# Keeping a bounded activation in PSUM, its high part on ACT, and an order planned with the port that DVE and GpSimd share

## Chip, cores and metric

The kernel runs on one core of a Trainium2 chip. The metric is the device time of one execution in microseconds, median of several runs; less is better.

## What is computed

Attention under a block-causal mask, and behind it two feed-forward layers on its output: the first with a quadratic bounded activation, the second with a leaky ReLU.

```python
# q, k, v: (4, 8, 576, 64); w_in: (512, 2048), w_out: (2048, 512) in each layer
scores = np.matmul(q, k.transpose(0, 1, 3, 2)) / np.sqrt(64)
mask = (pos[:, None] // 64) >= (pos[None, :] // 64)
scores = np.where(mask, scores, -1e9)
attn = softmax(scores) @ v
x = attn.transpose(0, 2, 1, 3).reshape(2304, 512)

h = x @ moe_w_in                      # layer 0
g = np.where(h >= 1, h, np.where(h <= -1, 0.0, (h + 1) ** 2 / 4))
x = g @ moe_w_out

h = x @ moe2_w_in                     # layer 1
g = np.maximum(0.01 * h, h)
out = g @ moe2_w_out                  # (2304, 512)
```

The weights are read as 64-bit words that the kernel itself converts to 32-bit floats.

## The kernel before

**Split operands.** In the two layers every operand stands as a high part (rounded to the fp32r type) and a low part (what the rounding left), and a product is three matmuls: high by high, low by high, high by low. A step therefore needs of each activation g the tiles gh and gl, and of each weight its two parts in the tile w.

**Tiles and stages.** Tokens are worked in blocks: layer 0 has seven of 256 and one of 512 tokens, layer 1 four of 512 and one of 256. The hidden dimension of 2048 is cut into 16 chunks of 128. A step of `moe_block` takes one chunk for 512 tokens or two for 256, so that its h is always one PSUM bank of 128x512. A block of 256 tokens has 8 steps, one of 512 has 16. In each step PE computes h (L579: 24 matmuls of 256 columns or 12 of 512) and, behind it, the step before's part of the output y (L618 in layer 0, L625 in layer 1). Between the two the activation is made: in layer 0 by ACT (L589 Relu of half of h and a half, L591 its square) and DVE (L592, the smaller of that and of max(h, 1), into g), in layer 1 by ACT (L596, 0.01 h) and DVE (L598, the maximum, into g). Then POOL copies g rounded into gh (L600) and DVE subtracts gl = g - gh (L602). The tile g is in SBUF and has one buffer, gh and gl have two. h uses bank 4 in the first block and banks 4 and 5 by turns afterwards.

**Weights.** For each half of a weight tile (512 columns; two halves a chunk, 32 a layer) `w_float` loads 512 KB of 64-bit words to wraw, ACT makes one part in PSUM (L318), POOL the sign part wsg in SBUF (L319), DVE joins the low words with wsg (L321, both inputs in SBUF) and then the whole (L331, one input in PSUM). `w_hi` rounds it into w on ACT (L286), and `w_lo` subtracts the low part (L294) on DVE for every other half and on POOL for the rest. The weight tiles of layer 1 take the places of those of layer 0 one by one, from the step on in which layer 0's last block has used them for the last time, so this conversion runs beside that block. The conversion of layer 0's weights runs beside the first attention units and the first block.

**Attention.** 32 units, in halves a and b of 16 pairs of heads: scores (L450, L465), the softmax on DVE (L367 negated maximum, L370 its scaling, L380 and L382 the reciprocal of the sums), ACT (L376 exponential) and POOL (L387 scaling of the rows), transposes on PE (L510) copied out by ACT and DVE (L515, L517), and the product with v (L526). Four units come before layer 0; the rest runs between the steps of its blocks 0 to 6.

**Order.** Nothing is issued as it is written. Each operation is put into a `Plan` with an engine, a cost, a priority and what it reads and writes. `schedule` plays the plan through, taking on each engine the ready operation of the lowest priority value, with the latencies of `DELAY` between engines, and emits the instructions in the order of that play. On the chip each engine then works strictly in that order. The plan of before has one resource per engine and nothing between engines but dependencies. At the start 14 matmuls on a zero tile (L352) keep PE busy until the first queries have come.

Of the kernel before, what the change touches and what calls it, by code (L numbers as in the profile page):

```python
# [34 lines left out]
          [(0, 512), (512, 512), (1024, 512), (1536, 512), (2048, 256)])  # L35
N_WARM = 14

W1_LO = ("dve", "pool")
W2_LO = ("dve", "pool")
NPRE = 3  # L40

# [9 lines left out]
    "POOL": {"PE": 150, "ACT": 70, "DVE": 70, "POOL": 10, "SP": 1250},  # L51
    "SP": {"PE": 2100, "ACT": 2000, "DVE": 2000, "POOL": 2000, "SP": 2800},
}


# [40 lines left out]
class Op:  # L96
    __slots__ = ("eng", "cost", "prio", "fn", "deps", "succ", "need", "ready", "seq", "end", "start")


class Plan:  # L100
# [8 lines left out]

    def op(self, eng, cost, prio, fn, r=(), w=()):  # L110
        o = Op()
        o.eng, o.cost, o.prio, o.fn, o.seq = eng, cost, prio, fn, len(self.ops)
        o.deps = {}
# [31 lines left out]
    def schedule(self):  # L145
# [7 lines left out]
        free = {e: 0 for e in engines}  # L153
        events = []
        for o in self.ops:
# [3 lines left out]
        while events:  # L159
# [5 lines left out]
            for e in engines:  # L165
                if free[e] <= t and waiting[e]:
                    _, _, o = heapq.heappop(waiting[e])
                    o.start, o.end = t, t + o.cost
                    free[e] = o.end
                    heapq.heappush(events, (o.end, 1, o.seq, None))  # L170
                    done.append(o)
                    for s in o.succ:
                        if s.deps[o]:
                            s.ready = max(s.ready, o.end + DELAY[e][s.eng])
                        else:
                            s.ready = max(s.ready, t)
                        s.need -= 1
                        if s.need == 0:
                            heapq.heappush(events, (max(s.ready, t), 0, s.seq, s))
# [10 lines left out]
def fused_kernel(ctx, tc, qk, v, w1, w2, out):  # L190
# [28 lines left out]

    def dve(cols, prio, fn, r, w, rate=1.042, fixed=68):  # L220
        plan.op("DVE", fixed + rate * cols, prio, fn, r, w)

    def pool(cols, prio, fn, r, w, fixed=161):
        plan.op("POOL", fixed + 0.95 * cols, prio, fn, r, w)

# [62 lines left out]

    def w_lo(prio, layer, fc, half, src, view, eng="dve"):
        t = W[layer, fc]  # L290
# [6 lines left out]
        if eng == "dve":  # L297
            dve(512, prio, f, *rw)
        else:
            plan.op("POOL", 1225, prio, f, *rw)  # L300

    def w_float(prio, layer, fc, half, hs, keep=None):
# [11 lines left out]
        def upper():  # L314
# [7 lines left out]
            sg.get().bitcast(I32), words()[:, :, 0], 29, sg.get().bitcast(I32),  # L322
            op0=ALU.logical_shift_right, op1=ALU.bitwise_or), [raw, sg], [sg])
        part = None
# [26 lines left out]
    for i in range(N_WARM):  # L351
        pe(427, -1000, lambda: nc.tensor.matmul(  # L352
            zp.get()[:, 0:128], lhsT=wz.get(), rhs=wz.get(), start=True, stop=True), [wz], [zp])

    def softmax(prio, tag, s, parts):

# [4 lines left out]
        for c, heads, view, _, _ in ((p[0], p[2], p[3], p[4], p[5]) for p in parts):  # L361
# [8 lines left out]
        dve(n, prio, lambda: nc.vector.tensor_scalar(nm.get()[:, 0:n], nm.get()[:, 0:n], SCALE, None, op0=ALU.mult),  # L370
            [nm], [nm])
        i = 0
        for c, _, heads, view, probs, pbufs in parts:
# [6 lines left out]
        dve(n, prio, lambda: nc.vector.tensor_scalar(rs.get()[:, 0:n], sm.get()[:, 0:n], 1e-9, None, op0=ALU.add),  # L380
            [sm], [rs])
        dve(8, prio, lambda: nc.vector.reciprocal(rs.get()[:, 0:n], rs.get()[:, 0:n]), [rs], [rs])  # L382
# [175 lines left out]
    def moe_block(layer, i, p0, dp, hbanks, ybanks):  # L558
# [8 lines left out]
        for t in range(NFC // nf + 1):  # L567
            pr = p0 + dp * nf * t
            if t < NFC // nf:
# [17 lines left out]
                if layer == 0:  # L587
# [3 lines left out]
                    act(512, pv, lambda gt=gt: nc.scalar.activation(gt.get(), gt.get(), AF.Square), [gt], [gt], sb=True)  # L591
                    dve(512, pv, lambda ps=ps, gt=gt: nc.vector.scalar_tensor_tensor(gt.get(), ps.get(), 1.0, gt.get(),  # L592
                                                                                     op0=ALU.max, op1=ALU.min),
                        [ps, gt], [gt])
                else:
                    act(512, pv, lambda ps=ps, gt=gt: nc.scalar.activation(gt.get(), ps.get(), AF.Copy, scale=0.01),  # L596
                        [ps], [gt])
                    dve(512, pv, lambda ps=ps, gt=gt: nc.vector.tensor_tensor(gt.get(), ps.get(), gt.get(), op=ALU.max),  # L598
                        [ps, gt], [gt])
                pool(512, pv, lambda gt=gt, gh=gh: nc.gpsimd.tensor_scalar(gh.get(), gt.get(), 1.0, 1.0, op0=ALU.mult,  # L600
                                                                           op1=ALU.mult), [gt], [gh])
                dve(512, pv, lambda gt=gt, gh=gh, gl=gl: nc.vector.tensor_tensor(gl.get(), gt.get(), bc(gh.get()),  # L602
                                                                                 op=ALU.subtract), [gt, gh], [gl])
            if pend is not None:
# [87 lines left out]
    for fc in range(NFC):  # L692
        w_tile(0, fc)
        for half in range(2):
# [4 lines left out]
            w_hi(pr, 0, fc, half, src, view, eng == "pool")  # L699
            w_lo(pr, 0, fc, half, src, view, eng)  # L700
    t = T_MOE
# [17 lines left out]
    for fc in range(NFC):  # L719
# [3 lines left out]
        for half in range(2):  # L723
# [3 lines left out]
            w_hi(g - 20, 1, fc, half, src, view, True)  # L727
            w_lo(g - 20, 1, fc, half, src, view, W2_LO[half])
    for i, (_, tb) in enumerate(BLOCKS[1]):
# [45 lines left out]
```

## Time and profile before

| | us |
|---|---|
| median of 3 runs (1051.5 to 1051.89) | 1051.72 |
| the profiled execution | 1051.97 |
| span of its instructions | 1050.0 |
| PE busy | 1013.1 (96%) |
| DVE busy | 485.9 (46%) |
| ACT busy | 349.2 (33%) |
| POOL busy | 294.9 (28%) |

All rows come from that one profiled execution. Busy time of PE is modelled, since matmuls are pipelined: the spacing of the starts says more than the length of one. A row of a group of instructions ends with the idle time of the engine just before them and with what ended most of it; idle time of an engine that nobody waits for costs nothing.

### The profile page before, as it was taken

The numbers are of one execution on the slowest core, as the hardware profiler recorded it, in microseconds if no ns is written. First come the engines' busy times: TensorE is split into PE (matmuls) and PEld (weight loads), VectorE is DVE, ScalarE is ACT, GpSimd is POOL, SyncE is SP. The second block draws the span as 40 slices with busy tenths as digits, with TensorE's granted clock in tenths as the row PEclk, the third lists the DMA queues.
The fourth block names the chain that finished last, engine by engine and source line by source line (L and its number), as shares of the span: only waits on it lengthen the run. The fifth ranks groups of instructions, "written<-read, shape, count | busy, mean of one in ns | idle before, by whom it ended". The sixth has DMA issues, their size and how long they took to land.

```text
span 1050.0 us, 16243 instructions
## 1 busy us (share of the span) xinstructions
PE 1013.1 (96%) x6300; PEld 852.6 (81%) x6300; DVE 485.9 (46%) x960; ACT 349.2 (33%) x776; POOL 294.9 (28%) x486
## 2 busy tenths in 40 slices
PE   6699899999999999999999899999999999999998
PEld 4487688888998889988987667888888888888897
DVE  5888855555245553345337987222222222222222
ACT  4666644444234443243325564011101101110110
POOL 4766532333113321022116774011011011101100
PEclk8999999999999999999999999999999999999999
DMA  6756443232312323112245565002100300200010
GB/s 193 220 184 215 154 143 109 72 112 73 124 57 73 104 81 114 43 56 97 96 155 186 183 197 201 2 0 81 41 1 1 120 1 1 81 0 1 1 42 20
DMA packets 53292, 95.41 MB, mean 91 GB/s; under 512 B 4832, under 2 KB 32480, under 8 KB 53216
## 3 DMA queue, kind: packets, MB, share of 16 engines
q1 hardware_dynamic: 53216, 94.39, 27.7%
q8 instruction: 49, 0.80, 0.3%
q14 instruction: 27, 0.22, 0.1%
HBM read 71.83 MB, written 22.54 MB: 90 GB/s over the span
## 4 chain that ended last, share of the span: by engine, by line
PE 83%; DVE 6%; issue 3%; POOL 3%; ACT 3%; DMA 1%; SPq 0%; DVEq 0%; ACTq 0%; POOLq 0%
PE bank L579 34%; PE slot L618 15%; PE slot L625 11%; PE bank L625 9%; PE slot L510 5%; PE slot L526 5%; PE slot L450 3%; DVE wsg L321 2%; PE slot L465 1%; DMA wraw<-w 1%; POOL w L294 1%; POOL wsg L319 1%; DVE gl L602 1%; ACT w L286 1%; DVE wpre L331 1%
## 5 line engine op out<-in xcount | busy, mean ns | idle before, releaser
L579 PE MATMUL bank<-xa,w 128*128 128x256 f32 (+1 forms) x1920 | 299.3, 308 | 4.2 <-DVE g L592 2.9
L579 PEld LDWEIGHTS bank<-xa,w 128*128 128x128 f32 x1920 | 262.8, 190 | 36.3 <-issue 13.5
L600 POOL TENSOR_SCALAR gh<-g 128x512 fp32r<-128x512 f32 x144 | 93.2, 647 | 532.2 <-DVE g L598 331.0
L618 PE MATMUL slot<-gh,w 128*128 128x256 f32 (+1 forms) x960 | 169.1, 296 | 1.1 <-POOL gh L600 0.7
L596 ACT ACTIVATE g<-bank 128x512 f32<-128x512 f32 x72 | 43.0, 597 | 342.1 <-PE bank L579 342.1
L598 DVE TENSOR_TENSOR g<-bank,g 128x512 f32<-128x512 f32 x72 | 49.8, 692 | 230.8 <-ACT g L596 230.8
L618 PEld LDWEIGHTS slot<-gh,w 128*128 128x128 f32 x960 | 133.8, 189 | 14.9 <-issue 9.5
L602 DVE TENSOR_TENSOR gl<-g,gh 128x512 fp32r<-128x512 f32 x144 | 107.7, 748 | 74.1 <-POOL gh L600 73.9
L579 PE MATMUL bank<-xb,w 128*128 128x512 f32 x576 | 141.9, 395 | 0.0
L579 PEld LDWEIGHTS bank<-xb,w 128*128 128x128 f32 x576 | 108.2, 188 | 25.7
L618 PE MATMUL slot<-gl,w 128*128 128x256 f32 (+1 forms) x480 | 104.1, 293 | 8.9 <-DVE gl L602 8.9
L625 PE MATMUL slot<-w,gh 128*128 128x512 f32 x320 | 100.4, 395 | 0.0
L592 DVE SCALAR_TENSOR_TENSOR g<-bank,g 128x512 f32<-128x512 f32 x72 | 49.6, 689 | 107.4 <-ACT g L591 107.1
L618 PEld LDWEIGHTS slot<-gl,w 128*128 128x128 f32 x480 | 75.0, 189 | 14.4 <-DVE gl L602 13.4
L625 PE MATMUL bank<-w,gh 128*128 128x512 f32 x256 | 80.5, 396 | 0.0
L589 ACT ACTIVATE g<-bank 128x512 f32<-128x512 f32 x72 | 43.0, 597 | 113.0 <-PE bank L579 102.8
L387 POOL TENSOR_SCALAR pb<-pb,rsb 128x448 f32<-128x448 f32 (+1 forms) x64 | 47.7, 754 | 99.9 <-DVE rsb L382 85.5
L625 PEld LDWEIGHTS slot<-w,gh 128*128 128x128 f32 x320 | 59.8, 189 | 13.2
L625 PE MATMUL slot<-w,gl 128*128 128x512 f32 x160 | 63.0, 394 | 0.0
L376 ACT ACTIVATE pb<-slot,nmb 128x448 f32<-128x448 f32 (+1 forms) x64 | 43.5, 684 | 55.1 <-DVE nmb L370 54.8
L319 POOL TENSOR_SCALAR wsg<-wraw 128x512 f32<-128x512 f32 x64 | 53.2, 831 | 23.5 <-DMA wraw<-w 10.9
L625 PEld LDWEIGHTS bank<-w,gh 128*128 128x128 f32 x256 | 48.1, 188 | 11.5
(77 smaller groups left out, 1149.9 us busy)
## 6 DMA issues: line engine op xcount, KB each, us to landing
wraw<-w SPq DMA_DIRECT2D x64, 512.0 KB, 4.0
x2d<-yt SPq DMA_DIRECT2D x36, 256.0 KB, 2.4
qkb<-qk SPq DMA_DIRECT2D x16, 416.0 KB, 3.6
xa<-x1d SPq DMA_DIRECT2D x12, 512.0 KB, 4.5
qka<-qk SPq DMA_DIRECT2D x16, 320.0 KB, 3.3
vb<-v SPq DMA_DIRECT2D x16, 320.0 KB, 2.9
out<-yo SPq DMA_DIRECT2D x18, 256.0 KB, 2.1
x1d<-xpb SPq DMA_DIRECT2D x16, 256.0 KB, 2.9
```

What stands on the lines that cost most here:

```text
L319: pool(512, prio, lambda: nc.gpsimd.tensor_scalar(sg.get(), upper(), 2.0 ** -126, 2.0 ** -126, op0=ALU.mult, op1=ALU.mult), [raw], [sg], f ...
L376: act(keys, prio, lambda view=view, probs=probs, k=k, i=i: nc.scalar.activation(probs[k](), view()[:, k], AF.Exp, bias=nm.get()[:, i:i + 1 ...
L387: pool(keys, prio, lambda probs=probs, k=k, i=i, rows=rows: nc.gpsimd.tensor_scalar(probs[k]()[0:rows], probs[k]()[0:rows], rs.get()[0:row ...
L510: nc.tensor.transpose(s.get()[:, hd, o:o + 128], pr.get()[:, hd, a:a + 128], ident.get())
L526: nc.tensor.matmul(s.get()[64 * hd:64 * hd + 64, 0, q0:q0 + m], lhsT=vt.get()[:, j, 64 * hd:64 * hd + 64], rhs=pts[i].get()[:, hd, o:o + m ...
L579: nc.tensor.matmul(ps.get()[:, j * tb:(j + 1) * tb], lhsT=win(layer, fc, p, kc), rhs=xt.get()[:, x, kc, 0:tb], start=(k == 0 and kc == 0 a ...
L592: dve(512, pv, lambda ps=ps, gt=gt: nc.vector.scalar_tensor_tensor(gt.get(), ps.get(), 1.0, gt.get(), op0=ALU.max, op1=ALU.min), [ps, gt], ...
L598: dve(512, pv, lambda ps=ps, gt=gt: nc.vector.tensor_tensor(gt.get(), ps.get(), gt.get(), op=ALU.max), [ps, gt], [gt])
L600: pool(512, pv, lambda gt=gt, gh=gh: nc.gpsimd.tensor_scalar(gh.get(), gt.get(), 1.0, 1.0, op0=ALU.mult, op1=ALU.mult), [gt], [gh])
L602: dve(512, pv, lambda gt=gt, gh=gh, gl=gl: nc.vector.tensor_tensor(gl.get(), gt.get(), bc(gh.get()), op=ALU.subtract), [gt, gh], [gl])
L618: nc.tensor.matmul(y[o].get()[:, e * tb:(e + 1) * tb], lhsT=wout(0, fc, p)[:, ec * 128:ec * 128 + 128], rhs=x.get()[:, j * tb:(j + 1) * tb ...
L625: nc.tensor.matmul(y[o].get(), lhsT=x.get()[:, j * tb + o * 128:j * tb + o * 128 + 128], rhs=wout(1, fc, p), start=(fc == 0 and k == 0), s ...
```

## The change

For every step but those of the first block, the bounded h is written by DVE back into the PSUM bank that h came in (`g is ps`), ACT makes gh from there with a Copy, and DVE's gl reads that bank and gh. In the first block (i = 0 of layer 0) g goes to SBUF and POOL makes gh, as before. In layer 1 all blocks take the new way.

The plan gets a resource that POOL and DVE share: operations marked `port` start when both their engine and the port are free. Marked are all of POOL but its memsets, and on DVE L321, L370, L380, the low part of weights whose source is in SBUF, and gl where g is in SBUF.

Besides, the number of warm-up matmuls goes from 14 to 10, a dummy exponential is put on ACT at the start, the plan lets SP begin at 1.5 us, and it expects 2.6 us from a DMA to the engines that wait for it.

```diff
-N_WARM = 14
+N_WARM = 10
+G_PSUM = 1
-    "SP": {"PE": 2100, "ACT": 2000, "DVE": 2000, "POOL": 2000, "SP": 2800},
+    "SP": {"PE": 2600, "ACT": 2600, "DVE": 2600, "POOL": 2600, "SP": 2800},
 }
+SP_START = 1500
...
-        events = []
+        port = 0
+        free["SP"] = SP_START
+        events = [(SP_START, 1, -1, None)]
...
-                    o.start, o.end = t, t + o.cost
+                    o.start = max(t, port) if o.port else t
+                    o.end = o.start + o.cost
+                    if o.port:
+                        port = o.end
...
     def pool(cols, prio, fn, r, w, fixed=161):
-        plan.op("POOL", fixed + 0.95 * cols, prio, fn, r, w)
+        plan.op("POOL", fixed + 0.95 * cols, prio, fn, r, w, fixed != 200)
...
+    dummy = Buf(plan, "dummy", 1, lambda: const.tile([128, 8], F32, name="dummy"))
+    act(8, -1000, lambda: nc.scalar.activation(dummy.get(), wz.get()[:, 0:8], AF.Exp), [wz], [dummy], extra=1280)
...
-                    dve(512, pv, lambda ps=ps, gt=gt: nc.vector.scalar_tensor_tensor(gt.get(), ps.get(), 1.0, gt.get(),
-                                                                                     op0=ALU.max, op1=ALU.min),
-                        [ps, gt], [gt])
+                    g = ps if i >= G_PSUM else gt
+                    dve(512, pv, lambda ps=ps, gt=gt, g=g: nc.vector.scalar_tensor_tensor(
+                        g.get(), ps.get(), 1.0, gt.get(), op0=ALU.max, op1=ALU.min), [ps, gt], [g])
                 else:
+                    g = ps
...
-                    dve(512, pv, lambda ps=ps, gt=gt: nc.vector.tensor_tensor(gt.get(), ps.get(), gt.get(), op=ALU.max),
-                        [ps, gt], [gt])
-                pool(512, pv, lambda gt=gt, gh=gh: nc.gpsimd.tensor_scalar(gh.get(), gt.get(), 1.0, 1.0, op0=ALU.mult,
-                                                                           op1=ALU.mult), [gt], [gh])
-                dve(512, pv, lambda gt=gt, gh=gh, gl=gl: nc.vector.tensor_tensor(gl.get(), gt.get(), bc(gh.get()),
-                                                                                 op=ALU.subtract), [gt, gh], [gl])
+                    dve(512, pv, lambda ps=ps, gt=gt: nc.vector.tensor_tensor(ps.get(), ps.get(), gt.get(), op=ALU.max),
+                        [ps, gt], [ps])
+                if g is ps:
+                    act(512, pv, lambda g=g, gh=gh: nc.scalar.activation(gh.get(), g.get(), AF.Copy), [g], [gh])
+                else:
+                    pool(512, pv, lambda g=g, gh=gh: nc.gpsimd.tensor_scalar(gh.get(), g.get(), 1.0, 1.0, op0=ALU.mult,
+                                                                             op1=ALU.mult), [g], [gh])
+                dve(512, pv, lambda g=g, gh=gh, gl=gl: nc.vector.tensor_tensor(gl.get(), g.get(), bc(gh.get()),
+                                                                               op=ALU.subtract), [g, gh], [gl], port=g is gt)
```

## Rows read from the trace of the kernel before

**Rows 1.** Busy time by stretch: stretch, its length, busy of each engine, granted clock, DMA.
```profile
0.00:130.00 130.00, 107.25 (x758) 84.52 (x759) 100.52 (x232) 80.65 (x197) 80.29 (x134) 0.93 0.61 193
...
165.00:540.00 375.00, 374.36 (x3037) 333.88 (x3036) 171.74 (x409) 143.71 (x344) 89.82 (x187) 1.00 0.27 87
540.00:641.00 101.00, 91.86 (x388) 70.76 (x387) 83.02 (x111) 53.94 (x94) 63.92 (x61) 0.98 0.59 188
641.00:1040.00 399.00, 399.00 (x1814) 327.77 (x1813) 109.10 (x158) 51.57 (x87) 47.69 (x74) 1.00 0.09 34
```

**Rows 2.** Timeline of PE, last block of layer 0: start, length, instruction, count.
```profile
537.58 2.94 PE L579 MATMUL bank<-xb,w 128*128 128x512 f32 x12
...
560.59 2.96 PE L579 MATMUL bank<-xb,w 128*128 128x512 f32 x12
...
566.19 2.96 PE L579 MATMUL bank<-xb,w 128*128 128x512 f32 x12
...
625.54 2.96 PE L579 MATMUL bank<-xb,w 128*128 128x512 f32 x12
...
635.40 2.95 PE L579 MATMUL bank<-xb,w 128*128 128x512 f32 x12
...
640.99 2.90 PE L579 MATMUL bank<-xa,w 128*128 128x512 f32 x12
```

**Rows 3.** Groups by line, 558 to 624 us: busy, mean ns, idle before.
```profile
L321 DVE SCALAR_TENSOR_TENSOR wsg<-wraw,wsg 128x512 int32<-128x512 int32 x24 | 19.8, 827 | 3.4 <-POOL wsg L319 3.2
L331 DVE SCALAR_TENSOR_TENSOR wpre<-bank,wsg 128x512 int32<-128x512 int32 x23 | 15.7, 684 | 1.4 <-ACT bank L318 0.5
L602 DVE TENSOR_TENSOR gl<-g,gh 128x512 fp32r<-128x512 f32 x10 | 12.2, 1222 | 0.5 <-POOL gh L600 0.5
L294 DVE TENSOR_TENSOR w<-wpre,w 128x512 fp32r<-128x512 f32 x10 | 8.9, 893 | 0.9 <-ACT w L286 0.8
...
L319 POOL TENSOR_SCALAR wsg<-wraw 128x512 f32<-128x512 f32 x23 | 21.0, 912 | 6.7 <-DVE wpre L331 4.8 <-DMA wraw<-w 0.5
L294 POOL TENSOR_TENSOR w<-wpre,w 128x512 fp32r<-128x512 f32 x12 | 19.1, 1594 | 6.9 <-ACT w L286 6.6
L600 POOL TENSOR_SCALAR gh<-g 128x512 fp32r<-128x512 f32 x10 | 8.8, 882 | 4.2 <-DVE g L592 2.3 <-PE bank L618 1.5
...
L589 ACT ACTIVATE g<-bank 128x512 f32<-128x512 f32 x11 | 6.5, 591 | 11.0 <-DVE gl L602 7.2 <-PE bank L579 3.8
```

**Rows 4.** Busy time of the same 66 us, as in rows 1.
```profile
558.00:624.00 66.00, 59.74 (x246) 45.11 (x245) 58.40 (x77) 39.06 (x69) 48.57 (x45) 1.00 0.60 190
```

**Rows 5.** Lines where little contends: ns min/median/max, first and last start (us).
```profile
L602 DVE TENSOR_TENSOR gl<-g,gh x73: 680/693/694, 641.8 to 1042.3; 128x512 fp32r<-128x512 f32 x73
L600 POOL TENSOR_SCALAR gh<-g x73: 617/618/626, 641.1 to 1041.6; 128x512 fp32r<-128x512 f32 x73
L319 POOL TENSOR_SCALAR wsg<-wraw x21: 641/661/1177, 51.4 to 127.6; 128x512 f32<-128x512 f32 x21
L294 POOL TENSOR_TENSOR w<-wsg,w x12: 1265/1284/1670, 50.0 to 130.6; 128x512 fp32r<-128x512 f32 x12
```

**Rows 6.** Timeline of one step of layer 1: gl, and PE's use of it.
```profile
807.58 0.69 DVE L602 TENSOR_TENSOR gl<-g,gh 128x512 fp32r<-128x512 f32 x1 [0.83 <-POOL gh L600]
...
810.82 0.63 PE L625 MATMUL slot<-w,gh 128*128 128x512 f32 x2
```

**Rows 7.** The start: the warm-up as a group, then timeline of PE and ACT.
```profile
L352 PE MATMUL bank<-wz 128*128 128x128 f32 x28 | 6.0, 409 | 1.0 <-DVE wz L349 1.0
...
6.95 1.91 PE L450 MATMUL slot<-qka 64*128 64x64 f32 x20
...
10.20 1.28 ACT L318 ACT_TABLE_LOAD   x1 [10.20 <-DMA wraw<-w]
...
12.38 0.31 ACT L376 ACTIVATE pa<-slot,nma 128x64 f32<-128x64 f32 x1 [0.26 <-DVE nma L370]
```

**Rows 8.** Waits of ACT, 165 to 540 us: total, times, longest.
```profile
ACT pb L376 <- DVE nmb L370: 48.9, 18, 4.2
```

More of the change, by code (lines that the diff above doesn't have):

```diff
@@ L96 @@
 class Op:
-    __slots__ = ("eng", "cost", "prio", "fn", "deps", "succ", "need", "ready", "seq", "end", "start")
+    __slots__ = ("eng", "cost", "prio", "fn", "deps", "succ", "need", "ready", "seq", "end", "start", "port")
 class Plan:
@@ L108, in __init__, with op @@
         self.regions = {}
-    def op(self, eng, cost, prio, fn, r=(), w=()):
+    def op(self, eng, cost, prio, fn, r=(), w=(), port=False):
         o = Op()
+        o.port = port
         o.eng, o.cost, o.prio, o.fn, o.seq = eng, cost, prio, fn, len(self.ops)
@@ L218, in act, with dve @@
         plan.op("ACT", (93 if sb else 51) + 0.833 * cols + extra, prio, fn, r, w)
-    def dve(cols, prio, fn, r, w, rate=1.042, fixed=68):
-        plan.op("DVE", fixed + rate * cols, prio, fn, r, w)
+    def dve(cols, prio, fn, r, w, rate=1.042, fixed=68, port=False):
+        plan.op("DVE", fixed + rate * cols, prio, fn, r, w, port)
     def pool(cols, prio, fn, r, w, fixed=161):
-        plan.op("POOL", fixed + 0.95 * cols, prio, fn, r, w)
+        plan.op("POOL", fixed + 0.95 * cols, prio, fn, r, w, fixed != 200)
     def dma(nbytes, prio, fn, r, w):
@@ L287, in w_hi, with w_lo @@
             [(t, (half * 2, half * 2 + 1))], sb=sb)
-    def w_lo(prio, layer, fc, half, src, view, eng="dve"):
+    def w_lo(prio, layer, fc, half, src, view, sb, eng="dve"):
         t = W[layer, fc]
@@ L297, in w_lo @@
         if eng == "dve":
-            dve(512, prio, f, *rw)
+            dve(512, prio, f, *rw, port=sb)
         else:
-            plan.op("POOL", 1225, prio, f, *rw)
+            plan.op("POOL", 1225, prio, f, *rw, True)
     def w_float(prio, layer, fc, half, hs, keep=None):
@@ L322, in w_float @@
             sg.get().bitcast(I32), words()[:, :, 0], 29, sg.get().bitcast(I32),
-            op0=ALU.logical_shift_right, op1=ALU.bitwise_or), [raw, sg], [sg])
+            op0=ALU.logical_shift_right, op1=ALU.bitwise_or), [raw, sg], [sg], port=True)
         part = None
@@ L370, in softmax @@
         dve(n, prio, lambda: nc.vector.tensor_scalar(nm.get()[:, 0:n], nm.get()[:, 0:n], SCALE, None, op0=ALU.mult),
-            [nm], [nm])
+            [nm], [nm], port=True)
         i = 0
@@ L380, in softmax @@
         dve(n, prio, lambda: nc.vector.tensor_scalar(rs.get()[:, 0:n], sm.get()[:, 0:n], 1e-9, None, op0=ALU.add),
-            [sm], [rs])
+            [sm], [rs], port=True)
         dve(8, prio, lambda: nc.vector.reciprocal(rs.get()[:, 0:n], rs.get()[:, 0:n]), [rs], [rs])
@@ L699, in fused_kernel @@
             w_hi(pr, 0, fc, half, src, view, eng == "pool")
-            w_lo(pr, 0, fc, half, src, view, eng)
+            w_lo(pr, 0, fc, half, src, view, eng == "pool", eng)
     t = T_MOE
@@ L727, in fused_kernel @@
             w_hi(g - 20, 1, fc, half, src, view, True)
-            w_lo(g - 20, 1, fc, half, src, view, W2_LO[half])
+            w_lo(g - 20, 1, fc, half, src, view, True, W2_LO[half])
     for i, (_, tb) in enumerate(BLOCKS[1]):
```

## The prediction

> **What bounds the kernel now.** I read the stages first, as one table of busy time by stretch [rows 1], because the share of the whole span (PE 96%) hides that the limits differ. From 165 to 540 us PE is busy 374.36 of 375 us, from 641 to 1040 us 399.00 of 399. In these 774 us nothing on ACT, DVE or POOL can be shortened to any use; a change there can only lose. PE has slack in two stretches. In the first 130 us (attention's first units and the conversion of the first layer's weights) it is busy 107.25 us at a mean granted clock of 0.93. From 540 to 641 us (last block of layer 0, while the second layer's weights are converted) it is busy 91.86 of 101 us, and DVE is busy 83.02.
>
> The second stretch, in order of time on PE [rows 2]: its h matmuls start at 537.58 us for the block's first step, and those of the next layer at 640.99, so 16 steps took 103.4 us. An unhindered step takes 566.19 - 560.59 = 5.60 us, 16 of them 89.6. **13.8 us are lost there.** From 566.19 to 625.54 nine steps took 59.35 us, 6.59 each; the last but one alone took 635.40 - 625.54 = 9.86.
>
> What ends last in those steps is gl. In the groups by line of 558 to 624 us [rows 3] the subtraction L602 takes 1222 ns, against 693 ns where no conversion runs [rows 5]; L321 takes 827 and L294 893. L331, which also runs on DVE but has one input in PSUM, takes 684, with no sign of a wait. POOL's operations stretch too: L319 912, L294 1594, L600 882, against 661, 1284 and 618 [rows 5]. So a DVE operation with two inputs in SBUF and a POOL operation hold each other up, and one with an input in PSUM is free of it. Taken as one resource, at the undisturbed durations, a step needs of it on POOL 2 x 0.661 + 1.284 + 0.618 = 3.22 us and on DVE four operations (L321 twice, L294, L602) of 0.69 = 2.77 us: **5.99 us for a step that PE could do in 5.60.** This is the bound of the stage. DVE is busy 58.40 us of these 66 [rows 4], ten steps of 5.84 us.
>
> A second tie shows in the ACT row of [rows 3]: L589 of the next step sat idle 7.2 us in ten steps for gl. The tile g has one buffer, ACT writes it first and gl reads it last, so the chain L589, L591, L592, L600, L602 of one step must end before that of the next begins.
>
> **The change, part by part.**
>
> *h in PSUM, its high part on ACT (all steps but the first block's 8, so 48 + 16 + 72 = 136).* In a conversion step L600 leaves POOL (0.618) and gl leaves the contended kind (0.69): the shared resource needs 5.99 - 0.62 - 0.69 = 4.68 us, 84% of a 5.60 us step. DVE keeps its eight operations: 5.84 us less 1.222 - 0.69 = 0.53 gives 5.31 us, still 95% of a step if L321 and L294 wait as long as now; they stand behind one POOL operation fewer, so I take about 5.1. ACT gains 0.60 us for each step (the Copy out of a bank; L589 takes 591 ns [rows 3]): 53.94 us of 101 [rows 1] become 63.5, still not the bound. And g is free once L592 has read it, so the loop over steps shrinks from five operations to three (0.59 + 0.62 + 0.68 = 1.9 us, L591 and L592 like the rows for L589 and L331). All three effects pull the same way.
>
> How much of 13.8 us comes back? The chain alone: gl shorter by 0.53 and the high part by 0.882 - 0.60 = 0.28 takes 0.8 from 6.59, which gives 5.8 a step, and 1.9 us lost in the nine steps instead of 8.9. By the shared resource or by DVE's work the step falls to PE's 5.60. I take 5.65 to 5.7 and leave some for the start of the block and stray waits: 2.5 us lost, **11.3 us gained** (bounds 5 and 13.4).
>
> What the change could cost: the bank is now freed by gl, not by L592. That binds nobody in this order, since the matmuls that reuse a bank stand on PE behind the y matmuls that need the same gl. In the PE-bound layer gl starts at 807.58 and the y matmuls that use it at 810.82 [rows 6]; an ACT Copy at 0.60 in place of a POOL operation at 0.62 changes that slack of over 2 us by almost nothing. So for the 72 + 48 steps of the PE-bound stretches I put **0**.
>
> [...]
>
> *Order planned with the shared resource.* The plan now makes POOL's operations (but for the memsets) and DVE's two-input SBUF ones take turns, and no longer believes that DVE and POOL get through 5.99 us in a step. It should put fewer conversions ahead of gl; they aren't urgent, as the second layer consumes one weight tile per 5.6 us step only from 640.99 on. Its worth is inside the 11.3; without it I would take 8 to 9.
>
> *The start: 4 warm-up matmuls fewer, the table loaded by a dummy, DMA expected later (SP from 1.5 us on, 2.6 us to others instead of 2.0 to 2.1).* The 28 warm-up records take 6.0 us, and the first scores start at 6.95, right as they end [rows 7]. Four matmuls are 8 records, 8 x 6.0/28 = 1.7 us. That is gained only if the first queries have landed by 5.3 us, which no row of PE shows; bounds 0 and 1.7, I take 1.2. ACT's first act is a weight: it waits until 10.20, loads the table in 1.28 us, converts 0.63 us, and starts the first exponential at 12.38 [rows 7], though the scores of 20 records were all there at 6.95 + 1.91 = 8.86. With the table loaded early and the first weight expected later, the plan should put the exponentials first. The scores and a reduction on DVE allow an exponential at about 9, some 3.5 us earlier. How much of these 1.2 + 3.5 us reaches the end? In the first 130 us DVE is busy 100.52 [rows 1], the most of any engine but PE; where it paces, work done earlier stays earlier, but conversions pushed back cost some of it. I take two thirds: **3.2 us gained**, bounds -4 (the new order pushes the conversions behind attention and the first block, which they pace, waits) and 7.
>
> *Sum.* The profiled execution took 1051.97 us (1050.0 of span, 1.97 around it), 0.25 above the median of 1051.72. 1051.97 - 11.3 - 3.2 = 1037.5, on the median's scale **1037.2 us**.
>
> **The rivals.**
>
> *A: DVE stays the bound of the conversion stage.* For it: 5.31 us of DVE work in a 5.60 us step, and DVE never got beyond 58.40/66 = 88% use [rows 4]. At 88% a step takes 6.0: nine steps lose 3.6 us instead of 8.9, the gain is 5.3. With 1.5 us from the start: 1045 us. Against it: the waits that hold DVE at 88% come from the very contention and loop that shrink.
>
> *B: the start brings all of it.* 13.4 from the conversion stage, 6 to 7 from the first 130 us, where PE also idles 22.75 us in all [rows 1]: 1031.5 us.
>
> *C: slower, since ACT becomes the one that ends last in blocks 1 to 6.* ACT's queue is in order, and there its exponentials stood idle for the negated maximum 48.9 us in 18 waits, 4.2 us at the longest [rows 8]. The high part now stands in that queue, and behind a stalled exponential it makes gl late and PE wait, in the stretch with nothing to give. POOL had no such waits in front of gh. Price: if half of it reached PE, 24 us, so 1061 us. It decides from 14.5/48.9 = 30% on. Against it: the mean wait is 2.7 us, about the slack that [rows 6] shows; L589 and L591 already stand in this queue; PE lost only 0.64 us in that stretch.
>
> *D: the new plan spoils the start.* The conversions fall behind, and the first block with them, by as much as the conversion stage gains: 1051 us. The same value holds if the change doesn't do what it says, because gl out of PSUM waits for POOL all the same; L331 speaks against that.
>
> **How the numbers follow.** Forecast 0.56 (its own range 1034 to 1042), A 0.18, B 0.12, C 0.05, D 0.09. The range must reach into A and B: 1031 to 1047.5 leaves out part of B, C and D. About 0.2% is what a measurement of this kernel can tell from no change, that is 1049.6 to 1053.8: forecast, A and B lie below it (0.86), D splits into 0.01 faster, 0.04 same and 0.04 slower, C is slower.
>
> **What will show it.** L602 at 0.69 us in all blocks but the first; h matmuls 5.6 to 5.7 us apart through the last block of layer 0; L600 in 8 instructions only; the first exponential before 10 us; the PE-bound layer with unchanged steps. I am wrong if the steps of the conversion stage stay above 6 us, if PE shows waits between 165 and 540 us, or if the last weight of the first layer is written later than now.

## The result, and the profile after

The changed kernel takes 1041.86 us (median of 4 runs, 1041.1 to 1043.1) against 1051.81 beside it: **0.990 of the time before, 95% interval 0.9879 to 0.9921.** Forecast were 1037.2 us; 9.95 us came where 14.5 were expected.

The stages first, as in [rows 1] (columns as there). The last block of layer 0 now ends at 631, so the third line covers 91 us where before it covered 101.

```profile
0.00:130.00 130.00, 106.01 (x739) 83.64 (x740) 100.56 (x236) 81.35 (x205) 76.92 (x136) 0.92 0.64 203
...
165.00:540.00 375.00, 374.83 (x3059) 334.96 (x3058) 171.03 (x409) 171.50 (x390) 59.35 (x139) 1.00 0.26 83
540.00:631.00 91.00, 90.57 (x404) 73.43 (x404) 71.49 (x103) 58.88 (x105) 38.01 (x41) 1.00 0.62 203
631.00:1030.00 399.00, 399.00 (x1813) 326.99 (x1812) 114.40 (x168) 96.42 (x165) 6.83 (x7) 1.00 0.11 38
```

PE has next to no idle time left in the conversion stage (90.57 of 91). In the first 130 us it is busy for 106.01, less than the 107.25 of before. ACT's 28 us more in the PE-bound 375 us cost PE nothing (374.83 against 374.36).

The timeline of PE, last block of layer 0 (start, length), answers [rows 2]: h matmuls of the first two steps, the last step, and the first of layer 1.

```profile
540.65 2.96 PE L594 MATMUL bank<-xb,w 128*128 128x512 f32 x12
546.29 2.96 PE L594 MATMUL bank<-xb,w 128*128 128x512 f32 x12
...
624.41 2.96 PE L594 MATMUL bank<-xb,w 128*128 128x512 f32 x12
630.90 2.95 PE L594 MATMUL bank<-xa,w 128*128 128x512 f32 x12
```

Cut at the first and the last of these starts, the profiled executions compare so:

| us | before | after | difference |
|---|---|---|---|
| start to first h of the last block of layer 0 | 537.58 | 540.65 | **+3.07** |
| that block, 16 steps | 103.41 | 90.25 | **-13.16** |
| layer 1, to the last matmul's start | 404.28 | 404.54 | +0.26 |
| span | 1050.0 | 1040.2 | -9.8 |

So the stage at which the change aims gave all that it had (16 ideal steps are 89.6), and a part of it had been lost before the stage was reached. Some 1.4 us of the 13.16 are clock (an estimate): before, PE waited 2.5 us for gl, up to 631.69 us, and its next eight matmuls started over 3.02 us, most of them 0.43 us apart, where they otherwise start 0.23 apart. The granted clock was 0.69 and 0.74 in the 3 us before and after 633, and 0.50 from 632 to 634.

The groups by line of 555 to 621 us answer [rows 3] (busy, mean ns, idle before).

```profile
L332 DVE SCALAR_TENSOR_TENSOR wsg<-wraw,wsg 128x512 int32<-128x512 int32 x22 | 19.1, 875 | 0.0
L342 DVE SCALAR_TENSOR_TENSOR wpre<-bank,wsg 128x512 int32<-128x512 int32 x22 | 15.1, 684 | 0.8
L305 DVE TENSOR_TENSOR w<-wpre,w 128x512 fp32r<-128x512 f32 x11 | 9.2, 836 | 0.9 <-ACT w L297 0.7
L621 DVE TENSOR_TENSOR gl<-bank,gh 128x512 fp32r<-128x512 f32 x12 | 8.2, 682 | 1.1 <-ACT gh L617 1.1
...
L330 POOL TENSOR_SCALAR wsg<-wraw 128x512 f32<-128x512 f32 x24 | 17.8, 741 | 22.1 <-DMA wraw<-w 12.6 <-DVE wpre L342 7.6 <-DVE wsg L332 0.7
L305 POOL TENSOR_TENSOR w<-wpre,w 128x512 fp32r<-128x512 f32 x11 | 14.7, 1337 | 19.1 <-ACT w L297 19.0
```

gl (L621) takes 682 ns instead of 1222, and POOL's two conversions take 741 and 1337 instead of 912 and 1594. The join on DVE (L332) is as stretched as before, 875: the contention is less, not gone. The start answers [rows 7] (timeline: start, length, what ended the idle time before it):

```profile
0.73 1.28 ACT L368 ACT_TABLE_LOAD   x1 [0.73 <-PEq L786]
...
5.62 2.24 PE L465 MATMUL slot<-qka 64*128 64x64 f32 x20
...
8.32 0.31 ACT L391 ACTIVATE pa<-slot,nma 128x64 f32<-128x64 f32 x1 [6.08 <-DVE nma L385]
```

The table is loaded while nothing else is to be done, the scores start 1.33 us earlier and the first exponential 4.06 us earlier than before; the first h starts at 37.58 instead of 43.65. All of this was gone again by 540 us.

### The profile page after: what moved, and what is told of

Read it like the earlier page. It is cut to its first block, busy times and chain, and to the rows that moved or that the text cites. A ratio compares the mean times of both kernels' runs of the same rounds, so it can differ in the third digit from the quotient of the medians.

```text
span 1040.2 us, 16155 instructions
## 1 busy us (share of the span) xinstructions
PE 1009.7 (97%) x6292; PEld 852.6 (82%) x6292; DVE 480.9 (46%) x960; ACT 427.6 (41%) x913; POOL 192.7 (19%) x350
## 4 chain that ended last, share of the span: by engine, by line
PE 91%; DVE 4%; ACT 3%; issue 1%; POOL 1%; DVEq 0%; ACTq 0%; POOLq 0%
PE bank L594 38%; PE slot L637 17%; PE slot L644 11%; PE bank L644 9%; PE slot L525 5%; PE slot L541 5%; PE slot L465 3%; PE bank L637 2%; PE slot L480 2%; DVE wsg L332 1%; ACT w L297 1%; ACT pa L391 0%; ACT pb L391 0%; PE bank L363 0%; POOL pa L402 0%
## 5 line engine op out<-in xcount | busy, mean ns | idle before, releaser
L594 PE MATMUL bank<-xa,w 128*128 128x256 f32 (+1 forms) x1920 | 303.7, 309 | 10.8 <-ACT w L297 7.3
L614 DVE TENSOR_TENSOR bank<-bank,g 128x512 f32<-128x512 f32 x72 | 50.4, 700 | 236.4 <-ACT g L612 236.4
L621 DVE TENSOR_TENSOR gl<-bank,gh 128x512 fp32r<-128x512 f32 x136 | 93.6, 688 | 64.3 <-ACT gh L617 64.0
L617 ACT ACTIVATE gh<-bank 128x512 fp32r<-128x512 f32 x136 | 81.2, 597 | 83.7 <-DVE bank L614 50.2
L608 DVE SCALAR_TENSOR_TENSOR bank<-bank,g 128x512 f32<-128x512 f32 x64 | 44.7, 698 | 102.1 <-ACT g L606 101.8
L402 POOL TENSOR_SCALAR pb<-pb,rsb 128x448 f32<-128x448 f32 (+1 forms) x64 | 44.9, 710 | 231.2 <-DVE rsb L397 206.2
L604 ACT ACTIVATE g<-bank 128x512 f32<-128x512 f32 x72 | 43.1, 598 | 87.0 <-PE bank L594 85.3
L330 POOL TENSOR_SCALAR wsg<-wraw 128x512 f32<-128x512 f32 x64 | 47.1, 736 | 81.4 <-DMA wraw<-w 67.7
```

The source lines that it names most:

```text
L330: pool(512, prio, lambda: nc.gpsimd.tensor_scalar(sg.get(), upper(), 2.0 ** -126, 2.0 ** -126, op0=ALU.mult, op1=ALU.mult), [raw], [sg], f ...
L402: pool(keys, prio, lambda probs=probs, k=k, i=i, rows=rows: nc.gpsimd.tensor_scalar(probs[k]()[0:rows], probs[k]()[0:rows], rs.get()[0:row ...
L594: nc.tensor.matmul(ps.get()[:, j * tb:(j + 1) * tb], lhsT=win(layer, fc, p, kc), rhs=xt.get()[:, x, kc, 0:tb], start=(k == 0 and kc == 0 a ...
L608: dve(512, pv, lambda ps=ps, gt=gt, g=g: nc.vector.scalar_tensor_tensor(g.get(), ps.get(), 1.0, gt.get(), op0=ALU.max, op1=ALU.min), [ps, ...
L614: dve(512, pv, lambda ps=ps, gt=gt: nc.vector.tensor_tensor(ps.get(), ps.get(), gt.get(), op=ALU.max), [ps, gt], [ps])
L617: act(512, pv, lambda g=g, gh=gh: nc.scalar.activation(gh.get(), g.get(), AF.Copy), [g], [gh])
```

## The experiments

Two theories stood against each other for each of the two stages. For the conversion stage: the contention between gl and the conversions was the bound (the prediction's view), or the order and the queues were. For the start: the loss comes from the later transfers in the plan, from the port in the plan, or is scatter from run to run. All runs in one table; the ratio is to the kernel before on the same chip. "Reach" is the start of the first h of the last block of layer 0, "from there" the time from it to the last matmul's start, and "weights" the number of high parts of layer 0's weights written by 100 us; these three are of the one profiled execution. The runs come from four chips (the result, e1 to e4, e5 to e8, e9 to e12), on which the kernel before took 1051.81, 1053.55, 1051.51 and 1052.69 us; across these groups the ratios are to be compared, not the microseconds.

| run | h in PSUM | port in plan | warm-up, table | later transfers | us | ratio | reach | from there | weights |
|---|---|---|---|---|---|---|---|---|---|
| before | | | | | 1051.81 | 1 | 537.6 | 507.7 | 23 |
| e1 | x | | | | 1041.07 | 0.9889 | 536.2 | 497.8 | 23 |
| e2 | | x | | | 1042.42 | 0.9900 | 543.1 | 495.5 | 22 |
| e3 | | | x | x | 1051.69 | 0.9980 | 539.8 | 507.3 | 22 |
| e4 | x | | x | x | 1042.18 | 0.9896 | 536.3 | 498.7 | 22 |
| e5 | only ACT's gh | | | | 1043.17 | 0.9923 | 535.3 | 500.6 | 23 |
| e6 | x | | | x | 1044.64 | 0.9932 | 540.6 | 497.9 | 23 |
| e7 | x | | x | | 1038.09 | 0.9864 | 532.8 | 498.6 | 24 |
| e8 | x | from 500 us on | x | | **1034.92** | 0.9839 | 535.5 | 494.5 | 24 |
| e9 (the change) | x | x | x | x | 1041.93 | 0.9896 | 541.5 | 494.3 | 21 |
| e10 | x | x | x | | 1043.18 | 0.9915 | 541.9 | 495.3 | 21 |
| e11 | x | from 500 us on | x | x | 1037.82 | 0.9861 | 538.1 | 494.0 | 22 |
| e12 (as e8) | x | from 500 us on | x | | **1036.14** | 0.9844 | 531.8 | 495.1 | 25 |

"From there" repeats within 1.3 us for runs that plan this stage in one way. "Reach" scatters more: e8 and e12 are one program and differ by 3.7 us in it. The mean granted clock of their first 165 us differs too, 0.92 in e8 and 0.96 in e12.

**e1 to e4: the parts apart.** e1 is the kernel before with h in PSUM alone, e2 with the port in the plan alone, e3 with the new start alone, e4 the changed kernel without the port in the plan.

```diff
 # e1: nothing but G_PSUM = 1 and the lines of g, gh and gl
+                    g = ps if i >= G_PSUM else gt
 # e2: g stays in SBUF, gh on POOL
+                    o.start = max(t, port) if o.port else t
 # e3: g stays in SBUF, gh on POOL, no port
-N_WARM = 14
+N_WARM = 10
+SP_START = 1500
 # e4, against the changed kernel
-                    o.start = max(t, port) if o.port else t
+                    o.start = t
```

> The kernel before with the part in PSUM and the high part on ACT alone (from the second block on), order planned as before, start as before. Theory 1 (the conversion stage gains since gl and gh leave the resource that DVE and POOL share; the first stage loses by the new plan): the 16 steps of layer 0's last block take 90 to 93 us instead of 103.4, the block starts within 1.5 us of 537.6, 1039 to 1042 us in all. Theory 2 (the plan that knows of the shared resource brought the gain): the block still takes 98 us or more, 1046 us or more.

> The kernel before with the shared resource in the plan alone. Theory 1: the last block of layer 0 still takes 97 to 103 us, as the resource is needed for longer than a step, and it starts 3 to 9 us later than 537.6 since the conversions of the first layer's weights are put off; 1050 to 1059 us. Theory 2: the block takes 91 to 93 us, 1041 to 1045 us.

> The kernel before with the start alone: 10 warm-up matmuls, the dummy exponential, DMA expected later. Theory 1: the first exponential at 8.3 us, the first h matmuls some 5 us earlier, layer 0's last block starts 0 to 4 us before 537.6, the block itself stays at 101 to 104 us; 1047 to 1052 us. Theory 3 (the loss of the first stage comes from expecting DMA later, which puts the conversions off): the block starts at 540 us or later, 1054 us or more.

> The changed kernel with the shared resource taken out of the plan, all else kept. Theory 1: the last block of layer 0 starts 0 to 4 us before 537.6 and takes 90 to 93 us, 1036 to 1041 us, less than the changed kernel. Theory 2: the block takes 98 us or more. Theory 3: the block starts at 540 us or later, and the time is that of the changed kernel or more.

Measured: 1041.07 (0.9889, interval 0.9873 to 0.9905), 1042.42 (0.9878 to 0.9922), 1051.69 (0.9968 to 0.9993) and 1042.18 (0.9881 to 0.9911). Either of the two main parts alone brings the whole gain within the noise (the change has 0.990), and they don't add up: "from there" falls by 9.9 us with h in PSUM, by 12.2 with the port in the plan, by 12.9 with both. The start alone (e3) gains 0.2%. Theory 1 of the expectations missed in four places: e1's block took 93.5 us, just above its range, e2 gained, e3 reached the last block later than before and not earlier, and e4 was not below the changed kernel.

That e2 gains speaks against the prediction's reason. In e2 gl is as slow as ever while PE is busy 87.58 of the 87.65 us from the block's first h to layer 1's. One line on gl and one on the join of the weights (ns min/median/max, first and last start), first before, then e2, each from the first h of the last block of layer 0 to the first h of layer 1:

```profile
L602 DVE TENSOR_TENSOR gl<-g,gh x16: 679/1120/1782, 537.7 to 635.5; 128x512 fp32r<-128x512 f32 x16
...
L331 DVE SCALAR_TENSOR_TENSOR wpre<-bank,wsg x32: 675/680/692, 548.9 to 640.9; 128x512 int32<-128x512 int32 x32
```

```profile
L620 DVE TENSOR_TENSOR gl<-g,gh x15: 681/1134/1782, 543.2 to 626.2; 128x512 fp32r<-128x512 f32 x15
...
L342 DVE SCALAR_TENSOR_TENSOR wpre<-bank,wsg x26: 672/678/693, 554.4 to 630.6; 128x512 int32<-128x512 int32 x26
```

The median of gl is 1134 ns in e2, 1120 before. What differs is the order: before, all 32 halves of the second layer's weights were joined by the end of the block; e2 joins 26 there and 6 after layer 1's first h, where PE is as busy (58.70 of the 59 us from 641 to 700). The changed kernel leaves 5 (27 of 32 by 630.3 us). So the conversions need not keep step with the block. It isn't that gl itself is put ahead: from the start of g's last write (L592, in e2 L607) to the start of gl it is 2.3 us on the mean before and 2.4 in e2. From L589 (L603) to that write it is 2.2 us before and 1.9 in e2.

**e5: the high part on ACT, g in SBUF.** No write into PSUM, no port in the plan: gl keeps two SBUF inputs, and only POOL's gh goes to ACT.

```diff
-                pool(512, pv, lambda gt=gt, gh=gh: nc.gpsimd.tensor_scalar(gh.get(), gt.get(), 1.0, 1.0, op0=ALU.mult,
-                                                                           op1=ALU.mult), [gt], [gh])
+                if layer == 1 or i >= G_PSUM:
+                    act(512, pv, lambda g=g, gh=gh: nc.scalar.activation(gh.get(), g.get(), AF.Copy), [g], [gh], sb=True)
```

> The kernel before with one thing changed: from the second block on (and in layer 1) the high part of g is taken by ACT instead of GpSimd, and g stays in SBUF, so that gl still reads two SBUF tiles. No PSUM write, no port in the plan, the old start. Theory P (the stage of the W2 conversions was slow because gl and the conversions stand in each other's way at the port): gl keeps durations of 1.1 to 1.8 us beside GpSimd's conversions, the last block of layer 0 keeps at least 98 us of its 103.4, and the time is 1046 to 1050. Theory Q (it was slow because GpSimd had both the high part of g and its conversions, and the g loop waited for GpSimd's queue): the block falls to 91 to 95 us with gl as slow as before, and the time is 1039 to 1044, like the version with h in PSUM.

Measured: 1043.17 us (0.9923, 0.9906 to 0.9939), the block 96.28 us. The time is theory Q's, though the block is 1.3 us longer than its range; that gl would stay slow, in which both agreed, was wrong (the line on gl as above, in e5):

```profile
L620 DVE TENSOR_TENSOR gl<-g,gh x16: 678/693/1125, 535.3 to 628.4; 128x512 fp32r<-128x512 f32 x16
```

Median 693 ns, though it still reads two SBUF tiles. Taking gh off POOL alone gives 7.1 of e1's 9.9 us "from there"; g in PSUM, with which no gl of the block is longer than 693 ns (e1; up to 1125 in e5) and the tile g comes free earlier, gives the other 2.8.

**What held the stage before.** With e2 and e5 in mind the trace of before can be read again. First the resource that the plan calls port: DVE and POOL in one contended stretch of that trace (timeline: start, length).

```profile
595.43 0.69 DVE L321 SCALAR_TENSOR_TENSOR wsg<-wraw,wsg 128x512 int32<-128x512 int32 x1
595.48 1.13 POOL L600 TENSOR_SCALAR gh<-g 128x512 fp32r<-128x512 f32 x1
...
596.04 1.10 DVE L294 TENSOR_TENSOR w<-wpre,w 128x512 fp32r<-128x512 f32 x1
596.68 0.97 POOL L319 TENSOR_SCALAR wsg<-wraw 128x512 f32<-128x512 f32 x1
597.06 1.13 DVE L602 TENSOR_TENSOR gl<-g,gh 128x512 fp32r<-128x512 f32 x1
```

Start plus length gives the ends: 596.12, 596.61, 597.14, 597.65, 598.19. They come in turn, 0.49 to 0.54 us apart. The two engines do alternate, but each has the resource for about 0.5 us, not for the 0.62 to 0.69 of an undisturbed row. So it is over the whole block: wherever an operation of one engine began at least 0.3 us before one of the other ended, its end came 0.53 to 0.55 us after the other's on DVE, 0.48 to 0.52 on POOL for L319 and L600, and 1.12 to 1.17 for L294. A step's demand is then 4 x 0.54 on DVE and 2 x 0.51 + 0.48 + 1.16 on POOL: 4.82 us, 86% of PE's 5.60. The port was not full, though busy enough for its users to meet often.

What PE lacked is gl (waits of PE over the last block of layer 0: total, times, longest; before, e5, e1, the changed kernel; e2 has none):

```profile
PE slot L618 <- DVE gl L602: 8.0, 9, 2.5
PE slot L636 <- DVE gl L620: 2.5, 4, 0.9
PE slot L636 <- DVE gl L620: 1.9, 4, 0.6
PE slot L637 <- DVE gl L621: 0.4, 1, 0.4
```

What made gl late, by the trace, is the loop of the single tile g, the prediction's "second tie". Again the timeline of before, the five operations of one step and the first of the next:

```profile
598.29 0.60 ACT L589 ACTIVATE g<-bank 128x512 f32<-128x512 f32 x1 [2.15 <-DVE gl L602]
...
599.36 0.62 ACT L591 ACTIVATE g<-g 128x512 f32<-128x512 f32 x1
...
600.10 0.68 DVE L592 SCALAR_TENSOR_TENSOR g<-bank,g 128x512 f32<-128x512 f32 x1
...
601.66 1.12 POOL L600 TENSOR_SCALAR gh<-g 128x512 fp32r<-128x512 f32 x1
...
603.25 1.12 DVE L602 TENSOR_TENSOR gl<-g,gh 128x512 fp32r<-128x512 f32 x1
...
604.46 0.60 ACT L589 ACTIVATE g<-bank 128x512 f32<-128x512 f32 x1 [2.44 <-DVE gl L602]
```

From L589 to L589 it is 6.17 us, and in the same timeline the h matmuls start at 600.67 and 606.86, 6.19 apart: this loop is the step. From 598 to 632 us every L589 starts 0.1 us after the end of gl; earlier in the block 0.4 to 2.2 us pass between the two, so the loop is not the whole of every step. Of the 6.17 us 4.14 are the lengths of the five operations (0.60 + 0.62 + 0.68 + 1.12 + 1.12), about 0.93 of them stretching (gh and gl over 0.618 and 0.693); 2.03 are gaps between them, for the most part time in which the engine works at a conversion that was put ahead: 0.47 us on ACT ahead of L591, 0.88 on POOL ahead of L600, 0.47 on DVE ahead of L602. In the changed kernel the loop waits for PE, not for gl:

```profile
594.00 0.60 ACT L604 ACTIVATE g<-bank 128x512 f32<-128x512 f32 x1 [1.37 <-PE bank L594]
...
597.23 0.69 DVE L621 TENSOR_TENSOR gl<-bank,gh 128x512 fp32r<-128x512 f32 x1 [0.17 <-ACT gh L617]
...
599.58 0.60 ACT L604 ACTIVATE g<-bank 128x512 f32<-128x512 f32 x1 [1.85 <-PE bank L594]
```

L604 to L604 is 5.58 us, and 1.85 us ahead of the second one ACT stood idle for PE. Each part takes something out of the loop, ACT's high part the queue of POOL and the stretched gh, PSUM the reads of g by gh and gl, the port in the plan some of the work that stood ahead of g's last write. In the step shown it was over PE's step by 0.6 us only, and so each part alone could get most of it. This is read from the traces: no run gave g a second buffer, which would show it, and how much of e2's gain is the order within a step and how much the six halves put off was not told apart.

**e6 and e7: which part of the start.** Both are e1 with one half of the new start.

```diff
 # e6
-    "SP": {"PE": 2100, "ACT": 2000, "DVE": 2000, "POOL": 2000, "SP": 2800},
+    "SP": {"PE": 2600, "ACT": 2600, "DVE": 2600, "POOL": 2600, "SP": 2800},
+SP_START = 1500
 # e7
-N_WARM = 14
+N_WARM = 10
+    act(8, -1000, lambda: nc.scalar.activation(dummy.get(), wz.get()[:, 0:8], AF.Exp), [wz], [dummy], extra=1280)
```

> The kernel before with h in PSUM and ACT's high part (as in e1), and of the start only the planner's later transfers (SP_START 1500, a transfer's result 2600 ns later); 14 warm-up matmuls, no table load ahead, no port in the plan. Theory S (the first stage loses because a planner that expects transfers later puts the W1 conversions behind attention work): the last W1 weight is written at 134 us or later (130.6 with e1), first h of the last block 2 us or more after e1's 536.2, and 1042 to 1045. Rival N (the loss of the first stage is scatter of the transfers from run to run): last W1 weight at 131 to 133 us and 1039 to 1042.

> The kernel before with h in PSUM and ACT's high part (as in e1), 10 warm-up matmuls instead of 14 and the table load ahead; the planner's transfer times as before, no port in the plan. Theory S (only the later transfers in the plan cost time in the first stage): first exp at 8.3 to 9.5 us, last W1 weight at 128 to 132 us, first h of the last block 2 to 4 us before e1's 536.2, and the time 1037 to 1039.5. Rival N: the earlier first h is given back by 165 us as in the changed kernel, since the first block is bound by its conversions, and the time stays at 1040.5 to 1042.5.

Measured: e6 1044.64 us (0.9932, 0.9917 to 0.9946), e7 1038.09 (0.9864, 0.985 to 0.9879). Against e1's 0.9889 the shorter warm-up with the early table is worth -0.25% (2.6 us; the two intervals overlap at the edge), and the later transfers cost +0.43% (4.5 us). e6's last weight came at 132.2 us, not after 134, and it has as many weights by 100 us as e1: that the later transfers do harm was right, by the weights alone it isn't explained. Its first h starts at 46.28, 2.6 us after e1's, and over its first 130 us the granted clock was 0.91, with PE busy 106.6 us, against 0.94 (mean of four stretches by their length) and 106.9 in e1. Why the later transfers cost that stays open.

**e8: the port for the late stage alone.**

```diff
-                    o.start = max(t, port) if o.port else t
+                    o.start = max(t, port) if o.port and t > 500000 else t
```

> As e7, and the port in the plan for work from 500 us on alone, so that the first stage keeps its order. Theory S: first stage as e7; the last block of layer 0 takes 90 to 91 us instead of e1's 93.5, and the time is 1034.5 to 1037.5, below the changed kernel's 1041.9. Rival N (the start is bound elsewhere, but the port's order still helps late): 1038 to 1040. If the port in the plan adds nothing on top of h in PSUM: the same as e7 within 1 us.

Measured: 1034.92 us (0.9839, 0.9822 to 0.9855), 3.2 us below e7 on the same chip and, by the ratios, some 6 us below the changed kernel. "From there" is 494.5, as with the port everywhere.

**e9 to e12: later transfers or not, port everywhere or late.** Four kernels on one chip.

> The changed kernel again, beside the next three on one chip: later transfers in the plan, port in the plan over the whole program. Both theories: 1041 to 1043.

> The changed kernel with the old transfer times in the plan (SP_START 0, a transfer's result after 2000 to 2100 ns); the port in the plan over the whole program. Theory S (the later transfers alone spoil the first stage): 3 to 4.5 us below the changed kernel, 1037 to 1039, with the W1 weights done by 137 us. Theory T (the port in the plan spoils the first stage as well, since it lets g and the scores' work pass the conversions): 0 to 2.5 us below it, 1039.5 to 1042, and the last W1 weight at 138 us or later.

> The changed kernel with the port in the plan from 500 us on alone; the later transfers in the plan stay. Theory S: the first stage stays late, and the time is that of the changed kernel within 1.5 us (1040.5 to 1042.5). Theory T (each of the two costs the first stage 2 to 4 us): 2 to 3.5 us below the changed kernel, 1038 to 1040.

> The kernel of e8 again: old transfer times, port in the plan from 500 us on alone. Theory S: equal to e10 within 1.5 us. Theory T: 2 to 4 us below e10. Both: 1034 to 1037, 5 to 8 us below the changed kernel.

Measured: 1041.93 (1040.18 to 1042.9), 1043.18 (1041.95 to 1045.66), 1037.82 (1036.73 to 1038.7) and 1036.14 (1033.51 to 1038.08). Keeping the port out of the plan for the first 500 us is worth 4.1 us with the later transfers and 7.0 without; in both pairs the ranges don't touch. Going back to the old transfer times gains nothing with the port everywhere (e10 is not below e9). So theory S fell, and theory T's main point holds: **it is the port in the plan that spoils the first stage**, and the later transfers come second. The loss lies ahead of 165 us: from there to 530 us PE is busy 364.0 to 364.8 of 365 us in all four. T's sizes were too small: e10 lies above its range, and e12 is 7.0 us below e10 where it had 2 to 4. In e11 and e12 the later transfers' 1.7 us is inside the scatter; without the port at all they cost 3.4 (e4 against e7: 0.9896 against 0.9864) to 4.5 (e6).

By the ratios the port late alone gains 2.6 us (e8 against e7) to 3.7 (e11 against e4). The port everywhere gains nothing over e4 (e9: both 0.9896) and costs 5.4 us over e7 (e10).

How, is seen in part in the weights of layer 0. The low parts made by POOL (count, ns, first and last start), e9 and e11, then e10 and e12:

```profile
L305 POOL TENSOR_TENSOR w<-wsg,w x16: 1266/1282/1530, 17.9 to 144.7; 128x512 fp32r<-128x512 f32 x16
L305 POOL TENSOR_TENSOR w<-wsg,w x16: 1267/1283/1845, 22.5 to 138.3; 128x512 fp32r<-128x512 f32 x16
```

```profile
L305 POOL TENSOR_TENSOR w<-wsg,w x16: 1261/1280/1708, 21.5 to 139.4; 128x512 fp32r<-128x512 f32 x16
L305 POOL TENSOR_TENSOR w<-wsg,w x16: 1263/1272/1657, 20.5 to 127.5; 128x512 fp32r<-128x512 f32 x16
```

With the port in the plan from the start the last one comes 6.4 and 11.9 us later. In e9 PE then waits for weights, in e11 much less (waits of PE from 40 to 160 us: total, times, longest):

```profile
PE bank L594 <- ACT w L297: 7.2, 2, 3.7
PE bank L594 <- ACT w L297: 1.8, 2, 1.6
```

In e10 such waits are 1.3 us only. There PE is busy from 40 to 60 us for as long as in e12, but at a lower granted clock (busy times as in [rows 1]; e10, e12):

```profile
40.00:60.00 20.00, 16.20 (x84) 12.65 (x85) 13.91 (x31) 9.65 (x22) 12.14 (x17) 0.67 0.54 175
40.00:60.00 20.00, 15.99 (x122) 12.80 (x120) 18.01 (x40) 13.47 (x28) 14.18 (x18) 1.00 0.60 199
```

It gets 84 matmuls done instead of 122, at a mean granted clock of 0.67 instead of 1.00. In the 20 us before, PE had been busy 12.07 us in e10 and 13.07 in e12. DVE has 13.91 against 18.01, so it isn't busier, it is kept waiting. As in e2 conversions are put behind the work of the block, and here the block needs them at once. How the 4.1 and 7.0 us divide between waits and clock was not told apart.

## Why the prediction was right or wrong

The sign was right and the time inside the range, and inside the forecast's own 1034 to 1042, at its edge. It missed by 4.7 us, from errors of opposite sign: 6.3 at the start, -1.9 in the conversion stage, 0.3 in layer 1, each read from one profiled execution. That they cancel in part is luck.

- **The conversion stage: mechanism half right, size too small.** 11.3 us forecast, 13.2 measured. The steps are 5.57 to 5.64 us apart but for the last (6.49), as the list of signs had it, and what is left over 89.6 is 0.65 us instead of 2.5. The value without the port, "8 to 9", came as 9.0 (e4) to 9.9 (e1). (The chain alone, with 0.81 us off each of nine steps, would leave 1.7 us lost and not 1.9; the sum doesn't use it.)
- **"5.99 us for a step that PE could do in 5.60. This is the bound of the stage"** is the step that failed in the reasoning. It added undisturbed durations as if the resource were held for all of them; the ends of contended operations show 0.48 to 0.55 us (1.16 for POOL's L294), 4.82 us a step. And it took two conversions a step for given, where the second layer can do with the last of them later. By the trace of before the tie named second, the loop over the one tile g, was the one that bound, at least from 598 to 632 us; the stretching of gh and gl is a part of that loop, so contention did count, but not as a full port. The gain came out all the same, since all three effects pull on that loop, as the text said.
- **DVE as the bound (rival A)** fell: DVE is busy 54.93 of 66 us (83%, [rows 4] had 88%), and PE is not kept waiting. Its 5.31 us were too many as well: the 5.84 that it starts from hold 2.3 joins a step (L331 x23 in ten steps, [rows 3]), and a step at PE's pace comes with 1.9 (L342 x22 in 66 us), which leaves 4.7 us of DVE a step. (The eight operations of DVE in a step of two conversions are seven.) Busy time of the changed kernel's 66 us:

```profile
555.00:621.00 66.00, 66.00 (x286) 53.52 (x285) 54.93 (x79) 45.16 (x82) 31.92 (x35) 1.00 0.58 191
```

- **The start: rows right, price wrong in sign.** The first exponential came at 8.32 (about 9 forecast), the scores 1.33 us earlier (1.2). 3.2 us of gain were put down, 3.07 of loss were measured (3.9 in e9, the same program). Two steps failed. One is to put the plan's new resource "inside the 11.3", as if it acted on the conversion stage alone: the first stage has the same conversions on the same two engines, and there it costs 4.1 to 7.0 us (e9 to e12). The other is to count the later transfers among what makes the start shorter: without the port they cost 3.4 to 4.5 us. The early table and the shorter warm-up, the rest of that price, are worth 2.6 us (e7 against e1). The early exponential doesn't decide: in e12, the faster one, the first starts at 10.42 us.
- **Rival D, that the conversions fall behind and the first block with them,** is what happened, at a quarter of the price that it was given. The sign named for it, a last weight of layer 0 later than now, was there: 143.87 us against 130.59. It is one of the three by which the prediction said it would be wrong.
- **Rival B** (1031.5) needed both stages; with the first stage's order left alone e8 and e12 come to 1034.9 and 1036.1.
- **Rival C fell.** ACT's exponentials stand idle less for the negated maximum than before, and the high parts wait 0.9 us at most (waits of ACT, 165 to 540 us: total, times, longest; the first answers [rows 8]):

```profile
ACT pb L391 <- DVE nmb L385: 36.2, 19, 3.2
ACT gh L617 <- DVE bank L608: 27.9, 38, 0.9
```

- **The PE-bound stretches at 0** held (the 0.26 us are of single profiles): PE idles 0.17 us from 165 to 540 (0.64 before), and layer 1 took 0.26 us more.
- **gl at 0.69 us out of PSUM,** as the list of signs had it, held. In layer 1 (ns min/median/max, first and last start), gl and the maximum that is now written into the bank:

```profile
L621 DVE TENSOR_TENSOR gl<-bank,gh x71: 680/692/694, 642.4 to 1032.4; 128x512 fp32r<-128x512 f32 x71
...
L614 DVE TENSOR_TENSOR bank<-bank,g x71: 690/700/700, 641.1 to 1031.0; 128x512 f32<-128x512 f32 x71
```

gl takes 692 ns against 693 from SBUF [rows 5].

## What to carry to other kernels

When two engines stretch each other, look at the ends of their rows in one short stretch before adding up durations: the loop with one buffer, queued behind other work on every engine that it visits, may bind although no resource is full. A planner that learns of a contended resource changes the order wherever the resource is used, so price it in each stage, and above all where the work that it puts off is awaited; here the same rule gains 2.6 to 3.7 us late and loses 4 to 7 early. And where two remedies act on one loop, each alone may bring nearly all of it: test them apart before adding them up.

## What the runs showed of the hardware

- DVE with two SBUF inputs and POOL take turns at 0.48 to 0.55 us for 128x512 (1.12 to 1.17 for POOL's subtraction of two tiles), while their undisturbed rows are 0.62 to 0.69 us long (1.28 for that one).
- A DVE result written into PSUM takes 700 ns (L614), against 692 into SBUF before (L598): 8 ns.
- ACT, DVE and POOL start their instructions in the order of the plan: 615, 879 and 400 in the profiled execution of before, 752, 879 and 264 in that of the changed kernel (compared by their lines, memsets left out), none out of its place.
- gl with two SBUF inputs falls from 1120 to 693 ns (medians) when POOL no longer does the operation just ahead of it (e5); that it collided because POOL's next operation starts at the moment that gh ends (596.68 after 596.61 us) is argued from the timeline, not shown by a run of its own.
- One program reached its last block of layer 0 at 535.5 us in one profiled execution (e8) and at 531.8 in another (e12): single profiles of that stretch should not be compared below several us. The mean granted clock was 0.92 and 0.96 over the first 165 us; what set that was not tested.
